# Running sums of a softmax layer in banks taken per segment, VectorE exponentials from key tile 7 on, and transposes by DMA in the last layer

## The chip, the cores and the metric

The kernel runs on one core of a Trainium2 chip. The metric is device time in microseconds (us) from the first to the last instruction's end, the median of several executions. The core's engines are TensorE (PE; its weight loads are listed as PEld), VectorE (DVE), ScalarE (ACT), GpSimd (POOL) and SyncE (SP), which here only issues DMAs.

## What is computed

The input x has 2048 tokens of 512 features in bf16. Four layers follow each other, A, B, A, B, each with its own layer normalisation and a residual. A is softmax attention with 32 query heads of 16 features and a single key and value head. B is linear attention with 32 heads.

```python
def _A_ref(x, wq, wk, wv, wo):
    q = (x @ wq).reshape(B, S, H, Dh).transpose(0, 2, 1, 3)
    k = x @ wk
    v = x @ wv
    p = _softmax(jnp.einsum("bhqd,bkd->bhqk", q, k) * (Dh ** -0.5), axis=-1)
    o = jnp.einsum("bhqk,bkd->bhqd", p, v)
    return o.transpose(0, 2, 1, 3).reshape(B, S, H * Dh) @ wo

def _B_ref(x, wqkv, wo):
    q, k, v = ...                       # 32 heads of 16
    phi = lambda t: jnp.where(t > 0, t + 1, jnp.exp(t)) + 1e-6
    kv = jnp.einsum("bhsd,bhse->bhde", phi(k), v)
    z = phi(k).sum(over s)
    o = (phi(q) @ kv) / (phi(q) @ z + 1e-6)
    return o.reshape(B, S, D) @ wo

x = x + _A_ref(_layernorm(x), ...); x = x + _B_ref(_layernorm(x), ...)
x = x + _A_ref(_layernorm(x), ...); x = x + _B_ref(_layernorm(x), ...)
```

In layers 0 and 2 each has 32 x 2048 x 2048 exponentials, which are the bulk of the work. Layer 1 and layer 3 need a sum over all tokens before any output.

## The kernel before: how it is tiled and what sets the order

**Tiles.** Tokens are cut into 16 tiles of 128. A *block* is 128 keys by 512 (query, head) columns; for a query tile and a parity (`par`) there are 16 key tiles times four row groups j of 32 partitions, 64 blocks. A layer has 16 x 2 x 64 = 2048 blocks.

**Planner.** The class `Planner` (lines 36 to 313) runs once in Python while the program is written. Every operation is given to it with engines, a duration, a priority (lower first) and the buffers that it reads and writes; it plays them in model time, and the order in which it starts them on each engine is the order of that engine's instructions on the chip. There each engine works its list in order and waits for semaphores. Durations, latencies (`DTL` for DMA transposes) and limits on backlogs are constants in lines 340 to 389, so they set an order and not a time. PSUM banks and buffers are handed out by pools, in order of priority of those who wait.

**A block's way.** `act_stream` (line 913) forms groups. A QK matmul writes a block's scores to a bank (`qk_mm`, line 805, its matmul at line 807). Banks 0 to 2 and 3 to 5 are two *sets*. ScalarE takes two or three blocks of a set in one exponential into one of six `PT` buffers (line 973). VectorE gets single blocks: either the third of a set (`dve_split`, line 1039, when no bank of the pool is free) or one in a bank of its own (`dve_open`, line 1033). It makes an integer approximation of the exponential, one conversion per block (line 1049) and three shifted copies per four blocks (line 1080), whose four value matmuls with weighted values sum up to the exponential. Both functions ask for the flag of key tile `KGATE` (15): before it no block goes to VectorE. `dve_split` also looks at VectorE's planned backlog (`BLS` 1.4, `BLT` 4.0).

**Value rounds.** `pv_try` (line 833) takes up to four finished blocks of different j of the current segment and adds value times exponential to the bank `ACC` = 6 (line 861). A *segment* (`Seg`, line 316) is one query tile and parity with some key tiles: early ones, in `PASSES` and `LATE`, have few key tiles, the later ones all 16. A segment that has all its rounds is copied out by VectorE: `norms` (line 1092) copies or adds bank 6 to `sacc` (lines 1103, 1105), after which the next segment's first round may start. Its rows are then transposed (line 1122), divided (lines 1129, 1133), transposed again (by DMA for query tiles below 12, line 1153) and projected (`epilogue`).

**Pool of banks.** `banks` (line 475) holds 7, then 5, and before the exponentials start also 0 to 4. Bank 5 leaves for a set when key tile 15 exists. Layer normalisation, K, V, Q, norms, projections and `dve_open` share it.

**Filler.** Where TensorE is idle in the plan, `fill` (line 887) and `fill_lin` (line 789) add matmuls with zero or unused result, into the running sum's bank or a spare bank.

**Layers 1 and 3.** Tiles of x go on to layer B as they are done. When all 16 are in, `den` gives the denominators and `main(t)` (line 1370) the outputs: numerators on TensorE (line 1416), division on VectorE into `OB` (line 1420, `NOB` = 4 buffers), transposes of `OB` on TensorE (line 1435), the copy to `OTB` on ScalarE or VectorE (line 569), the projection (line 575) and the residual on VectorE (line 1448). `FARM` lists tiles whose transposes go by DMA (line 1427; none), `RESA` tiles whose residual is added by a matmul with the identity and copied by ScalarE (lines 1443 to 1445; none). In layer 3 `store` (line 1465) sends each tile out. Transposes and stores are all issued by SP.

The start of exponentials and the wait for keys, as they are:

```python
yield ("flag", ("K", L, 0))
yield ("flag", ("K", L, 1))
yield ("flag", ("Q", L, 0))
...
while any(("K", L, kt) not in pl.flags for kt in sg.kts) or ("Q", L, sg.t) not in pl.flags:
```

## Time and profile before

| what | value |
|---|---|
| three runs | 1558.03, 1553.24, 1557.19 us; median 1557.19 |
| the profiled execution's own time | 1556.79 us |
| its span | 1555.1 us, mean granted TensorE clock 0.996 |
| first exponential of layer 0 | at 13.65 us |
| last exponentials of layer 0 and first of layer 2 | about 736 and 759.5 us |
| key tiles 0 to 3 of layer 2 written, 4 to 7, last | about 756 to 775, 805, 869.9 us |
| last exponential of layer 2 | about 1507.5 us |
| layer 3's outputs (numerators to the last residual) | 1520.9 to 1552.7 us |

How to read the profile. Busy time is the time in which an engine ran an instruction. A group's line gives the line of the kernel, the engine, the operation, its output and input with shape, the count, then busy time and the mean of one in ns, and after the second bar the idle time of the engine just before such instructions and what ended it. In the busy time by stretch the columns are the stretch, its length, the busy time (and count) of PE, PEld, DVE, ACT and POOL, the granted clock of TensorE as a share of full speed, the share of DMA and GB/s. In a timeline the columns are start and duration in us, then the instruction, and in brackets how long the engine was idle before it and what it waited for. SPq is the queue of SP.

### The profile page before, as it was taken

The page shows a single profiled execution, that of the slowest core. Times are in us where ns is not written, and L with a number is a line of the kernel's source. Part 1 is how long each engine was busy: PE and PEld are TensorE (multiplying, and loading weights), DVE is VectorE, ACT ScalarE, POOL GpSimd, SP SyncE. Part 2 cuts the span into 40 slices and gives each one's busy share as a digit, 9 for nine tenths or more (in the row PEclk, how much of TensorE's full clock was granted, in tenths as well). Part 3 has the DMA queues.
Part 4 walks back from the last instruction along what each step waited for, and adds up shares of the span by engine and source line. Part 5 has one row for each costly group of instructions (what it writes and reads, how often), then busy time and mean ns, then how long its engine had stood idle before and what let it go on. Part 6 is the DMA issues. An engine that isn't in the chain of part 4 may idle for free.

```text
span 1555.1 us, 36056 instructions
## 1 busy us (share of the span) xinstructions
PE 1458.7 (94%) x14602; PEld 535.4 (34%) x14713; DVE 1448.3 (93%) x2707; ACT 1476.8 (95%) x1500; POOL 68.8 (4%) x122
## 2 busy tenths in 40 slices
PE   8998999999999999999999989999999999999999
PEld 4322332333333333333644323323333333333345
DVE  7999999999999999998676799999999999999977
ACT  8999999999999999999699999899999999999982
POOL 4000000000000000000111000000000000000000
PEclk9999999999999999999999999999999999999998
DMA  5100010000000000000000000000000000000001
GB/s 132 47 2 1 8 22 5 8 8 5 8 8 8 5 8 5 1 1 1 2 1 1 1 1 15 15 8 8 6 9 5 8 8 8 5 5 2 1 2 55
DMA packets 40435, 17.55 MB, mean 11 GB/s; under 512 B 34128, under 2 KB 39760, under 8 KB 40272
## 3 DMA queue, kind: packets, MB, share of 16 engines
q1 hardware_dynamic: 40272, 15.25, 4.2%
q8 instruction: 118, 1.93, 0.5%
q14 instruction: 45, 0.37, 0.1%
HBM read 5.28 MB, written 2.10 MB: 5 GB/s over the span
## 4 chain that ended last, share of the span: by engine, by line
PE 32%; issue 23%; DVE 23%; ACT 20%; POOL 1%; DMA 0%; SPq 0%; ACTq 0%; POOLq 0%; DVEq 0%
ACT PT L973 19%; DVE FB L1049 11%; PE ps L861 11%; PE ps L807 9%; DVE FB L1080 6%; PE ps L575 4%; PE ps L906 2%; PE ps L732 2%; PE ps L1122 1%; POOL rs L655 1%; DVE st L651 1%; DVE sacc L1103 1%; PE ps L793 1%; ACT phE L1205 1%; DVE xn L658 1%
## 5 line engine op out<-in xcount | busy, mean ns | idle before, releaser
L973 ACT ACTIVATE PT<-ps 128x1024 bf16<-128x1024 f32 (+1 forms) x1361 | 1424.5, 1180 | 19.9 <-PE ps L861 13.4
L1049 DVE TENSOR_SCALAR FB<-ps 128x512 int16<-128x512 f32 x1017 | 675.0, 686 | 23.5 <-PE ps L807 20.7
L807 PE MATMUL ps<-QT,KM 32*128 32x512 bf16 x4096 | 533.4, 384 | 46.8 <-ACT PT L973 27.9
L861 PE MATMUL ps<-FB,VW 128*32 128x512 bf16 x4068 | 530.4, 385 | 19.5 <-ACT PT L973 9.5
L861 PE MATMUL ps<-PT,V 128*32 128x512 bf16 x3079 | 513.0, 386 | 9.7 <-ACT PT L973 5.6
L1080 DVE TENSOR_SCALAR FB<-FB 128x2048 int16<-128x2048 int16 (+1 forms) x765 | 503.0, 683 | 0.9
L807 PEld LDWEIGHTS ps<-QT,KM 32*128 32x128 bf16 x4096 | 139.8, 91 | 445.3 <-ACT PT L973 203.8
L861 PEld LDWEIGHTS ps<-FB,VW 128*32 128x32 bf16 x4068 | 133.4, 94 | 219.5 <-issue 113.0
L861 PEld LDWEIGHTS ps<-PT,V 128*32 128x32 bf16 x3079 | 125.9, 94 | 111.8 <-issue 56.1
L906 PE MATMUL ps<-QT,V 128*32 128x512 bf16 (+6 forms) x568 | 131.0, 315 | 0.9 <-DVE FB L1049 0.9
L655 POOL TENSOR_TENSOR rs<-ve,mhalf 128x1 f32<-128x1 f32 x64 | 51.7, 811 | 1398.9 <-DVE ve L653 1386.0
L575 PE MATMUL ps<-wqkv,xnT 128*128 128x512 bf16 (+1 forms) x211 | 65.1, 368 | 3.9 <-issue 2.9
L906 PEld LDWEIGHTS ps<-QT,V 128*32 128x32 bf16 x568 | 44.1, 95 | 59.6 <-issue 39.3
L1103 DVE COPY sacc<-ps 128x512 f32<-128x512 f32 x64 | 43.8, 684 | 7.8 <-PE ps L861 7.6
L1205 ACT ACTIVATE phE<-ps 128x512 bf16<-128x512 f32 (+1 forms) x66 | 41.3, 625 | 6.6 <-PE ps L732 4.7
L1122 PE MATMUL ps<-identF,sacc 128*128 128x128 f32 x256 | 45.9, 291 | 1.5 <-DVE sacc L1103 0.8
L732 PE MATMUL ps<-xnT,wqkv 128*128 128x128 bf16 x512 | 44.3, 221 | 0.0
L651 DVE BATCH_NORM_STATS2 st<-x_sb 128x6 f32<-128x512 bf16 x60 | 40.8, 683 | 2.6 <-DMA x_sb<-in_A_x_dram 2.3
L1105 DVE TENSOR_TENSOR sacc<-sacc,ps 128x512 f32<-128x512 f32 x56 | 38.2, 682 | 2.4 <-PE ps L861 2.1
L732 PE MATMUL ps<-xnT,wq 128*128 128x128 bf16 x480 | 38.6, 224 | 0.0
L575 PEld LDWEIGHTS ps<-wqkv,xnT 128*128 128x128 bf16 x272 | 21.8, 97 | 44.9 <-issue 34.2
L732 PEld LDWEIGHTS ps<-xnT,wqkv 128*128 128x128 bf16 x512 | 29.1, 98 | 22.8 <-issue 19.4
(115 smaller groups left out, 671.1 us busy)
## 6 DMA issues: line engine op xcount, KB each, us to landing
out_dram<-x_sb SPq DMA_DIRECT2D x16, 128.0 KB, 1.7
x_sb<-in_A_x_dram SPq DMA_DIRECT2D x3, 512.0 KB, 6.1
wqkv<-in_B_wqkv_dram SPq DMA_DIRECT2D x1, 1536.0 KB, 7.5
xnT<-xn SPq DMA_TRANSPOSE x36, 2.4
x_sb<-in_A_x_dram SPq DMA_DIRECT2D x4, 128.0 KB, 2.2
wq<-in_A_wq_dram SPq DMA_DIRECT2D x1, 512.0 KB, 4.2
wo<-in_A_wo_dram SPq DMA_DIRECT2D x1, 512.0 KB, 4.1
wo<-in_B_wo_dram SPq DMA_DIRECT2D x1, 512.0 KB, 8.5
```

The lines of the kernel that those rows point to most:

```text
L575: return e.matmul(dst, lhsT=l, rhs=r, start=(k == 0), stop=(k == len(pairs) - 1))
L655: op({PO: (0.55, lambda e: e.tensor_tensor(out=rs[:, t:t + 1], in0=ve[:, t:t + 1], in1=mhalf[:], op=ALU.pow))}, reads=[("ve", t), "mhalf"] ...
L732: ins = e.matmul(dst[:, g * P:(g + 1) * P], lhsT=lhs(g, k), rhs=rhs(k), start=(k == 0), stop=(k == FT - 1))
L807: return e.matmul(bank(b), lhsT=KM[r, sg.par, kt * P:(kt + 1) * P], rhs=QT[r, sg.t, :], start=True, stop=True)
L861: ins = e.matmul(ps[32 * j:32 * j + 32, ACC * 512:(ACC + 1) * 512], lhsT=V[:, kt, :] if w is None else VW[:, kt, w, :], rhs=ap, start=(k = ...
L906: o = op({PE: (n / 2400.0, lambda e: e.matmul(ps[32 * j:32 * j + 32, b * 512:b * 512 + n], lhsT=V0[:], rhs=QT[:, sg.t, 0:n], start=st, sto ...
L973: ex = op({AC: (0.05 + 0.4267 * n, lambda e, n=n, s_=s_, p_=p_: e.activation(PT[:, p_, 0:n * 512], ps[:, s_ * 512:(s_ + n) * 512], ACTF.Ex ...
L1049: o = op({DV: (0.60, lambda e: e.tensor_scalar(out=dst.bitcast(I16), in0=bank(b), scalar1=VB, scalar2=VLO, op0=ALU.add, op1=ALU.max))}, wr ...
L1080: o = op({en: (du, lambda e, w=w, g_=g_: e.tensor_scalar(out=FB[:, g_, 0:n].bitcast(I16), in0=FB[:, f_, 0:n].bitcast(I16), scalar1=float(w ...
L1103: o = op({DV: (0.6, lambda e, src=src: e.tensor_copy(src, bank(ACC)))}, writes=[B_(ACC), key], prio=0.0, lat=0.15)
L1122: o = op({PE: (0.12, lambda e, c=c: e.transpose(ps[:, b * 512 + c * P:b * 512 + (c + 1) * P], src[:, c * P:(c + 1) * P], identF[:]))}, rea ...
L1205: op({AC: (0.07 + n / 1200.0, lambda e: e.activation(phE[:, i, 0:n], bank(b, n), ACTF.Exp))}, reads=[B_(b)], writes=[("phE", i)], prio=min ...
```

## The change

- `ACC` is gone. Bank 6 joins the pool `banks`. Each segment has its own `acc`, which `norms` takes from the pool at priority 0.2 when the segment before has at most `LOWV` = 12 value matmuls left (flag `low`) and the one before that has been copied out (flag `out`). `drain` copies it out and gives the bank back.
- `pv_try` builds a round out of finished blocks of two successive segments, in up to two banks. `fill` may write in either; `fill_lin` needs a free bank for which nobody waits.
- `KGATE` is 7 instead of 15. `act_stream` no longer waits for key tile 1 at the start, and per block for that block's key tile only, not for all of the segment.
- `DTL` is 2.7 instead of 4.0 and `BLT` 3.0 instead of 4.0.
- In layer 3 tiles 1 to 15 transpose by DMA, with buffers in `FB` in place of the four of `OB` and `OTB`, and odd tiles add the residual on TensorE and copy on ScalarE.
- For tile 15 in layers 1 and 3 the value part yields to the key part (`pr + 0.001` and a sleep of 0).

```diff
+LOWV = 12
-DTL = 4.0
+DTL = 2.7
-FARM = {1: (), 3: ()}
+FARM = {1: (), 3: tuple(range(1,16))}
-BLT = 4.0
+BLT = 3.0
-KGATE = 15
-RESA = {1: (), 3: ()}
+KGATE = 7
+RESA = {1: (), 3: tuple(range(1, 16, 2))}
...
-    ACC = 6
-    banks = Pool_([7] + list(GROW) + [b for b in SB if b not in GROW])
+    banks = Pool_([7, 6] + list(GROW) + [b for b in SB if b not in GROW])
...
     def fill_lin():
-        if lin["a"] or pl.busy[PE] or ("x", 3, T - 1) in pl.flags:
+        if lin["a"] or pl.busy[PE] or ("x", 3, T - 1) in pl.flags or not banks.free or banks.wait:
...
         def pv_try():
...
+            open_ = [s for s in segs[cur["i"]:cur["i"] + 2] if s.acc is not None and s.submitted < s.total]
             items, js = [], set()
-            for x in sg.ready:
-                if x[1] not in js and ("V", L, x[0]) in pl.flags:
-                    items.append(x)
-                    js.add(x[1])
+            for s in open_:
+                for x in s.ready:
+                    if x[1] not in js and ("V", L, x[0]) in pl.flags:
+                        items.append((s, x))
+                        js.add(x[1])
...
-                    ins = e.matmul(ps[32 * j:32 * j + 32, ACC * 512:(ACC + 1) * 512], lhsT=V[:, kt, :] if w is None else VW[:, kt, w, :], rhs=ap,
+                    ins = e.matmul(ps[32 * j:32 * j + 32, s.acc * 512:(s.acc + 1) * 512], lhsT=V[:, kt, :] if w is None else VW[:, kt, w, :], rhs=ap,
...
+            s = open_[0]
+            if s.total - s.submitted <= LOWV:
+                pl.flag(("low", L, s.i))
...
         def act_stream():
             yield ("flag", ("K", L, 0))
-            yield ("flag", ("K", L, 1))
             yield ("flag", ("Q", L, 0))
...
-                    while any(("K", L, kt) not in pl.flags for kt in sg.kts) or ("Q", L, sg.t) not in pl.flags:
-                        yield ("flag", next((("K", L, kt) for kt in sg.kts if ("K", L, kt) not in pl.flags), ("Q", L, sg.t)))
-                    else:
-                        group.append((sg,) + blk)
-                        continue
-                    sg.left.insert(0, blk)
-                    break
+                    for f in (("K", L, blk[0]), ("Q", L, sg.t)):
+                        while f not in pl.flags:
+                            yield ("flag", f)
+                    group.append((sg,) + blk)
...
         def norms():
+            yield ("flag", ("Q", L, 0))
+            yield ("flag", ("K", L, 0))
             for sg in segs:
-                pl.flag(("acc", L, sg.i))
+                if sg.i:
+                    yield ("flag", ("low", L, sg.i - 1))
+                if sg.i > 1:
+                    yield ("flag", ("out", L, sg.i - 2))
+                sg.acc = yield ("acq", banks, 0.2)
                 pl.at(pl.now, pv_kick)
+                pl.process(drain(sg))
+
+        def drain(sg):
+            yield ("flag", ("pv", L, sg.i))
+            if sg.i:
+                yield ("flag", ("out", L, sg.i - 1))
...
+            if sg.first:
+                o = op({DV: (0.6, lambda e, src=src: e.tensor_copy(src, bank(sg.acc)))}, writes=[B_(sg.acc), key], prio=0.0, lat=0.15)
+            else:
+                o = op({DV: (0.6, lambda e, src=src: e.tensor_tensor(out=src, in0=src, in1=bank(sg.acc), op=ALU.add))},
+                       writes=[B_(sg.acc), key], prio=0.0, lat=0.15)
+            if sg.last:
+                pl.process(norm(sg, src, key, a_))
+            pl.give_after(banks, sg.acc, [o])
+            pl.flag(("out", L, sg.i))
+            if sg.i == len(segs) - 1:
+                lin["a"] = False
...
         def crit_v(t, sl, pr):
-            bs = yield from acq2(pr)
+            bs = yield from acq2(pr + 0.001)
...
             if t in ECRIT:
                 pl.process(crit_k(t, sl, pr))
+                yield ("sleep", 0.0)
                 yield from crit_v(t, sl, pr)
...
+            if L == 3:
+                i = NOB + t
+                ob, otb = FB[:, t // 4, t % 4 * 512:t % 4 * 512 + 512], FB[:, 4 + t // 4, t % 4 * 512:t % 4 * 512 + 512].rearrange("p (g c) -> p g c", c=P)
+                fo, ft_ = [("FB", t // 4, t % 4)], [("FB", 4 + t // 4, t % 4)]
+            else:
+                i = yield ("acq", ob_pool, pr)
+                ob, otb, fo, ft_ = OB[:, i, :], OTB[:, i, :, :], [], []
...
             if t in FARM[L]:
-                dmat(OTB[:, i, :, :], OB[:, i, :], [("OB", i, 0), ("OB", i, 1)], [("OTB", i)], pr)
+                dmat(otb, ob, [("OB", i, 0), ("OB", i, 1)], [("OTB", i)], pr, after=ft_)
```

## The prediction

> **What bounds the kernel now.** I read the page's busy table and costliest groups first, then the busy time by stretch, then the waits of ScalarE, then the tail in order of time. The execution took 1556.79 us (span 1555.1); the median of the three runs is 1557.19, so the working below stands 0.4 us under the median.
>
> ```profile
> PE 1458.7 (94%) x14602; PEld 535.4 (34%) x14713; DVE 1448.3 (93%) x2707; ACT 1476.8 (95%) x1500; POOL 68.8 (4%) x122
> L973 ACT ACTIVATE PT<-ps 128x1024 bf16<-128x1024 f32 (+1 forms) x1361 | 1424.5, 1180 | 19.9 <-PE ps L861 13.4
> L1049 DVE TENSOR_SCALAR FB<-ps 128x512 int16<-128x512 f32 x1017 | 675.0, 686 | 23.5 <-PE ps L807 20.7
> L1080 DVE TENSOR_SCALAR FB<-FB 128x2048 int16<-128x2048 int16 (+1 forms) x765 | 503.0, 683 | 0.9
> ```
>
> Three engines are nearly full. The exponentials of both softmax layers are 4096 blocks of 128x512: ScalarE did 3079, VectorE 1017. A ScalarE block costs 1424.5/3079 = 0.463 us. A VectorE block costs (675.0+503.0)/1017 = 1.158 us, because it is converted once and shifted three times (four blocks per shift). Together they do 1/0.463 + 1/1.158 = 3.02 blocks per us, ScalarE 71% of them. So **a microsecond of ScalarE idle costs 0.71 us, one of VectorE idle 0.29 us, and a block moved into idle time saves 1/3.02 = 0.33 us**. These are the prices below; they hold while either engine can take any block.
>
> ```profile
> 29.50:39.60 10.10, 9.21 (x106) 4.59 (x109) 7.07 (x21) 10.10 (x10) 4.30 (x10) 1.00 0.58 166
> 806.00:870.00 64.00, 60.17 (x619) 27.77 (x625) 42.97 (x97) 63.48 (x58) 7.53 (x16) 1.00 0.01 1
> 970.00:1070.00 100.00, 94.83 (x913) 30.91 (x921) 99.40 (x184) 94.52 (x99) 3.60 (x4) 1.00 0.06 9
> 1520.80:1532.00 11.20, 10.98 (x95) 6.93 (x96) 6.63 (x10) 1.66 (x3) 0.00 (x0) 0.57 0.04 13
> 1541.00:1549.90 8.90, 8.85 (x80) 5.45 (x79) 8.68 (x17) 1.94 (x4) 0.00 (x0) 1.00 0.26 88
> ```
>
> Columns: stretch, length, busy PE, PEld, DVE, ACT, POOL, granted clock, DMA. In 806 to 870 ScalarE is full and VectorE idles 21.0 us: that is layer 2 before its last key tile exists. In 970 to 1070 VectorE is full and ScalarE loses 5.5 us. In the tail TensorE is full, at a clock of 0.57 at first.
>
> **Overlapping value rounds.** Now one bank holds the running sum: a segment's last value matmuls wait for late VectorE shifts, then VectorE copies the bank out, and only then may the next segment's value matmuls start. The worst place, in order of time:
>
> ```profile
> 972.68 1.04 PE L906 MATMUL ps<-QT,V 128*32 128x512 bf16 x4
> 973.97 0.69 DVE L1105 TENSOR_TENSOR sacc<-sacc,ps 128x512 f32<-128x512 f32 x1
> 974.72 0.40 PE L861 MATMUL ps<-FB,VW 128*32 128x512 bf16 x3
> 975.38 1.02 ACT L973 ACTIVATE PT<-ps 128x1024 bf16<-128x1024 f32 x1 [3.29 <-PE ps L861]
> ```
>
> TensorE plays filler (L906), the copy-out runs, value matmuls follow at once, and ScalarE, whose six result buffers were full, starts 3.29 us late. All such waits are the 13.4 us beside L973. With a second bank taken when 12 value matmuls of the old segment are left, the next segment's rounds go on. At full effect that is 13.4 x 0.71 = 9.5 us; at none 0. I take two thirds, **6.4 us**, since the longest ones have just this form and the short ones may be ordinary queueing. The copy-outs (0.68 us each, 120) stay. What is late next is a QK matmul: VectorE waits 20.7 us for L807, worth 5.9 us if all went; I count none of it.
>
> **VectorE from key tile 7 on.** Layer 2's key tile 7 is written at about 805.5, tile 15 at 869.9. The first limit is VectorE's idle time: three quarters of 21.0 us over 1.158 is 13.6 blocks. The second is TensorE, which idles 3.8 us there and fills 0.8: each such block adds three value matmuls at (530.4+513.0)/7147 = 0.146 us busy, so 10.5 blocks; a packed round of four starts every 0.215 us, which would allow 28. I take 12 blocks: **4.0 us** (0 to 6.0). Layer 0 has 3.0 us of idle VectorE at 29.5 to 39.6, two blocks, **0.7 us**. These blocks queue ahead of layer 1's VectorE work (0.5 before 1.5 and up); that work only has to bring key tiles 8 to 15 in time, and layer 2 then has 256 blocks ready on key tiles 0 to 7, of which about 100 are used by 806, so ScalarE does not run dry.
>
> **Starting on the first key tile.** ScalarE's first exponential starts at 13.65, though key tile 0 was ready at 9.1 and the first queries at 10.6; the start waited for tile 1. Four blocks need tile 0 only: 4 x 0.463 x 0.71 = 1.3 us per layer at most. They stand in ScalarE's queue before copies that layer 0 needs at 11.8 and layer 2 at 757 to 759, so I take half for both, **1.3 us** (-1 to 2.6).
>
> **The tail.** Per pair of tiles TensorE's part of the chain that ended last is 1.83 (projections) + 0.45 (transposes) + 0.45 (numerators) + 0.16 (filler) = 2.89 us:
>
> ```profile
> 1540.47 0.45 PE ps L1435 x8
> 1540.91 0.45 PE ps L1416 x8
> 1541.36 0.16 PE ps L793
> 1541.52 1.83 PE ps L575 x8
> ```
>
> SP's own instructions, min/median/max in ns, are these:
>
> ```profile
> L583 SPq DMA_TRANSPOSE OT<-Osb x24: 1189/1190/2209, 173.9 to 1337.1; - x24
> L1467 SPq DMA_DIRECT2D out_dram<-x_sb x16: 332/332/1102, 1527.6 to 1552.7; - x16
> ```
>
> After: no transposes and no need of filler, but one matmul with the identity for the odd tile (0.22): 1.83 + 0.45 + 0.22 = 2.50. Saved 0.39 x 7.5 pairs = 2.9 us. VectorE falls from 0.42 + 1.28 + 1.44 = 3.1 us of work per pair to 2.0. New is SP's queue, which the planner counts at 0.1 us each: 15 transposes at 1.19 and 16 stores at 0.33 are 23.2 us. Stores queue behind transposes whose tile is not ready, and later transposes behind stores. From the second tile's numerators at 1523.5 SP would end at 1546.7, before today's last store at 1552.7, so it does not set the end, but each first projection waits 2.4 us for a landing instead of one 0.59 us copy. I take off 0.9 us: **2.0 us** (4.6 if SP paced the end, -7 in a rival below).
>
> **Counted at nothing.** The DMA latency of 2.7 instead of 4.0 only reorders; transposes land in 2.4. The VectorE backlog limit of 3.0 instead of 4.0 is covered by VectorE being 95 to 99% busy; each per cent of idle it made over 1400 us would cost 14 x 0.29 = 4.1 us. The order of tile 15's K and V evacuations moves tenths. Filler now needs a free bank with nobody waiting; where that fails, the clock is at stake.
>
> Sum: 6.4 + 4.0 + 0.7 + 1.3 + 2.0 = 14.4; 1556.8 - 14.4 = **1542.4 us**.
>
> **Rivals.**
> - *All stalls go* (0.17): 9.5 + 6.0 + 0.7 + 2.6 + 4.6 and the 5.9 us of QK waits, 29.3, gives **1527.5**. For it: the same stalls feed each other. Against: TensorE is at 94%.
> - *The order does not overlap in fact* (0.13): the instruction order is fixed from the planner's durations, which are short (0.60 against 0.664 for L1049), so the stalls stay and TensorE admits few extra blocks: 2.0 + 0.7 + 0.6 is left, **1553.5**.
> - *The tail stays at half clock* (0.07). The clock drops to 0.50 at 1523 and recovers at about 1532, after projections ran without a gap. At half clock eight projection matmuls took 3.43 us; a tile is then 1.72 + 0.45 + 0.22 = 2.4 us, 16 of them 38 against today's 31: the tail loses 7 and the time is **1551.4**. A proof against it: projections, once fed, fill TensorE at that clock (2.4 us per tile against 1.5 from SP), as in the stretch that ended the drop before. The Trainium skill, TensorE: Matmul & The Clock Gate, "Why this matters for your kernels", warns of idle gaps above about 3 us between bursts of matmuls, each returning the clock to half. This trace dropped with TensorE 98% busy, on matmuls 8 columns wide, so a busy share alone does not rule it out; by that rule a wait for transposes would count too, and the sum would be 1551.4 instead of 1542.4.
> - *Bank shortage* (0.17), the slower one. After a layer's last query tile only banks 6 and 7 serve everything but exponentials. While both hold running sums, norms, output projections and the next layer's K, V and Q wait. ScalarE's groups of two (1004 of 1361) are formed mostly when bank 7 is not free, so it is taken some 70% of the time; of the 45 us per token tile 13.5 are spare. It decides once two sums overlap for over 13.5/2 = 6.7 us per segment (the case above shows 4). Then the next layer falls a tile behind: K, V and Q of a tile take 2.5 + 1.5 + 2.8 = 6.9 us, twice 13.7. With the overlap's gain gone, 1556.8 + 13.7 - 8.0 = **1562.5**.
>
> **Chances.** Forecast 0.46, the rivals as given. A difference under 0.3% (4.7 us) cannot be told from none here. Faster: 0.46 + 0.17 + 0.03 of the second and 0.03 of the third = 0.69; same 0.14; slower 0.17. The range, 1527 to 1562, reaches from the full gain to the shortage and leaves out about half of each.
>
> **What would show it.** Overlap right: idle of L973 before value matmuls falls from 13.4 to about 4 us, and less filler. Key gate right: L1049 from about 806 on, VectorE over 85% busy in 806 to 870, some 14 more VectorE blocks in all. Tail right: no L1435 but for tile 0, about 2.5 us per pair, the last store near 1538. Wrong: copy-outs of running sums late with idle ScalarE behind them, a longer stretch between layers, transposes on SP back to back up to the end, or a clock of 0.5 beyond ten microseconds.

## The result, and the profile after

The changed kernel takes 1563.22 us (median of 20 runs, 1555.18 to 1570.17), the kernel before in the same series 1556.49 (20 runs, 1552.34 to 1558.06). The ratio is 1.0046, 95% interval 1.0032 to 1.0059: **slower by 6.7 us**, where 14.4 us less had been forecast. The profiled execution took 1562.38 us (span 1560.5, mean granted clock 0.991; before 1555.1 and 0.996).

What the change was to do, it did. From the page, the busy table and the groups of the exponentials (in the order of the lines shown of before):

```profile
PE 1477.1 (95%) x14568; PEld 532.9 (34%) x14676; DVE 1455.5 (93%) x2723; ACT 1474.9 (95%) x1538; POOL 70.7 (5%) x122
L967 ACT ACTIVATE PT<-ps 128x1024 bf16<-128x1024 f32 (+1 forms) x1398 | 1418.4, 1135 | 11.7 <-PE ps L807 6.5
L1043 DVE TENSOR_SCALAR FB<-ps 128x512 int16<-128x512 f32 x1034 | 688.3, 684 | 24.1 <-PE ps L807 20.2
L1074 DVE TENSOR_SCALAR FB<-FB 128x2048 int16<-128x2048 int16 x780 | 513.2, 678 | 0.7
```

VectorE did 17 blocks more (1034 for 1017). ScalarE's idle time before exponentials fell from 19.9 to 11.7 us, and value matmuls, which had been behind 13.4 of it, are behind 3.6 in its waits:

```profile
ACT PT L967 <- PE ps L807: 6.5, 17, 0.8
ACT PT L967 <- PE ps L857: 3.6, 9, 0.9
```

The same stretches as before, by engine (length, PE, PEld, DVE, ACT, POOL, granted clock, DMA): VectorE now works 55.61 us of 806 to 870 (42.97 before), and in 970 to 1070 ScalarE is full (99.83, 94.52 before).

```profile
806.00:870.00 64.00, 61.03 (x546) 21.86 (x548) 55.61 (x113) 62.13 (x67) 7.13 (x11) 1.00 0.01 1
970.00:1070.00 100.00, 98.57 (x998) 34.72 (x997) 98.39 (x182) 99.83 (x99) 2.71 (x3) 1.00 0.07 12
1520.80:1532.00 11.20, 10.96 (x109) 7.79 (x110) 7.97 (x13) 0.59 (x1) 0.00 (x0) 0.53 0.38 68
```

Where the gain went is seen by cutting the two executions at the same events, in us:

| event | before | after | part's change |
|---|---|---|---|
| last exponential of layer 0 ends | 736.2 | 730.9 | -5.3 |
| first exponential of layer 2 | 759.5 | 756.7 | +2.5 |
| last exponential of layer 2 ends | 1507.98 | 1498.7 | -6.5 |
| first denominator of layer 3 | 1519.12 | 1520.10 | **+10.3** |
| end of the span | 1555.1 | 1560.5 | **+4.4** |

Up to layer 0's last exponential and within layer 2's exponentials, 11.8 us are saved in this execution, where 12.4 were forecast for overlap, gate and start. That the two agree is luck. The experiments e1, e2, e13 and e18 below have the changed kernel's order of instructions in layer 0, and there its last exponential ends at 736.4 to 737.5 us, later than before. What repeats is the stretch from the 200th of layer 0's 2048 blocks to the last: 639.5 to 640.5 us in these five executions, 645.0 before. The first 200 blocks took 90.8 us here but 96.4 to 97.7 in the other four (91.2 before). And part of layer 2's 6.5 us is work put off: the stretch behind its exponentials is 10.3 us longer, and layer 3's outputs lose 4.4 more.

ScalarE behind layer 2's last exponential, in order of time, first after:

```profile
1487.86 10.84 ACT L967 ACTIVATE PT<-ps 128x1024 bf16<-128x1024 f32 x10
1498.55 0.63 ACT L1271 CAST va<-ps 128x512 bf16<-128x512 f32 x1
1500.83 0.60 ACT L1212 ACTIVATE phE<-ps 128x512 bf16<-128x512 f32 x1 [1.65 <-PE ps L732]
...
1506.56 1.16 ACT L1212 ACTIVATE phE<-ps 128x512 bf16<-128x512 f32 x2
...
1513.58 0.60 ACT L1212 ACTIVATE phE<-ps 128x512 bf16<-128x512 f32 x1 [1.50 <-PE ps L732]
1515.33 1.64 ACT L1212 ACTIVATE phE<-ps 128x256 bf16<-128x256 f32 x4 [1.16 <-DVE QT L1215]
1516.83 0.68 ACT L1243 CAST va<-ps 128x256 bf16<-128x256 f32 x2
1517.87 0.60 ACT L1212 ACTIVATE phE<-ps 128x512 bf16<-128x512 f32 x1 [0.35 <-PE ps L732]
```

and before, where four such operations (L1205 there) are all that is left:

```profile
1494.20 13.77 ACT L973 ACTIVATE PT<-ps 128x1536 bf16<-128x1536 f32 x12
1507.77 0.69 ACT L1263 CAST va<-ps 128x512 bf16<-128x512 f32 x1
1510.82 0.60 ACT L1205 ACTIVATE phE<-ps 128x512 bf16<-128x512 f32 x1 [2.36 <-PE ps L732]
```

`phE` is the feature map of layer 3's queries and keys, one operation per tile for each and two for the last tile's keys; the queries' matmul (L732) needs a bank. In the changed kernel 8 of these operations fall in 760 to 1300 (20 before) and 15 behind 1490 (4 before), where no exponentials hide them. Of layer 3's 16 query tiles 13 come behind the last exponential, 2 before.

What lengthens the outputs is, as e13 will show, the work of SP, whose list holds the transposes and the stores of layer 3 in one order:

```profile
1524.03 5.64 SPq L583 DMA_TRANSPOSE FB<-FB  x4
1529.76 0.54 SPq L1482 DMA_DIRECT2D out_dram<-x_sb  x1
1530.39 1.19 SPq L583 DMA_TRANSPOSE FB<-FB  x1
1533.54 4.46 SPq L1482 DMA_DIRECT2D out_dram<-x_sb  x4
1538.27 5.00 SPq L583 DMA_TRANSPOSE FB<-FB  x3
1543.36 0.53 SPq L1482 DMA_DIRECT2D out_dram<-x_sb  x1
1543.94 6.43 SPq L583 DMA_TRANSPOSE FB<-FB  x5
...
1554.28 3.96 SPq L1482 DMA_DIRECT2D out_dram<-x_sb  x8
```

Five transposes have gone by 1531.6. Then four stores stand first in the list and wait for projections, which run at a clock of 0.53 in 1520.8 to 1532; the other ten transposes come behind them, from 1538.27 on: ten at 1.19 us and three stores at 0.53 are 13.5 of the 15.9 us up to 1554.2, so hardly a pause is left.

### The profile page after: what moved, and what is told of

It is laid out like the page before. It is cut to its first block, busy times and chain, and to the rows that moved or that the text cites. A ratio compares the mean times of both kernels' runs of the same rounds, so it can differ in the third digit from the quotient of the medians.

```text
span 1560.5 us, 36074 instructions
## 1 busy us (share of the span) xinstructions
PE 1477.1 (95%) x14568; PEld 532.9 (34%) x14676; DVE 1455.5 (93%) x2723; ACT 1474.9 (95%) x1538; POOL 70.7 (5%) x122
## 4 chain that ended last, share of the span: by engine, by line
PE 43%; DVE 22%; ACT 18%; issue 15%; DMA 1%; POOL 1%; SPq 0%; ACTq 0%; POOLq 0%; DVEq 0%
ACT PT L967 17%; PE ps L857 15%; PE ps L807 13%; DVE FB L1043 10%; DVE FB L1074 7%; PE ps L575 4%; PE ps L904 4%; PE ps L732 2%; PE ps L1129 2%; DVE sacc L1108 1%; DMA FB<-FB 1%; POOL rs L655 1%; DVE st L651 1%; DVE QT L1215 1%; DVE sacc L1215 0%
## 5 line engine op out<-in xcount | busy, mean ns | idle before, releaser
L967 ACT ACTIVATE PT<-ps 128x1024 bf16<-128x1024 f32 (+1 forms) x1398 | 1418.4, 1135 | 11.7 <-PE ps L807 6.5
L1043 DVE TENSOR_SCALAR FB<-ps 128x512 int16<-128x512 f32 x1034 | 688.3, 684 | 24.1 <-PE ps L807 20.2
L857 PE MATMUL ps<-FB,VW 128*32 128x512 bf16 x4136 | 581.7, 386 | 12.1 <-ACT PT L967 7.9
L807 PE MATMUL ps<-QT,KM 32*128 32x512 bf16 x4096 | 547.9, 384 | 34.3 <-ACT PT L967 13.6
L857 PE MATMUL ps<-PT,V 128*32 128x512 bf16 x3062 | 548.7, 387 | 9.5 <-ACT PT L967 6.5
L1074 DVE TENSOR_SCALAR FB<-FB 128x2048 int16<-128x2048 int16 x780 | 513.2, 678 | 0.7
L857 PEld LDWEIGHTS ps<-FB,VW 128*32 128x32 bf16 x4136 | 142.1, 94 | 206.3 <-issue 106.7
L904 PE MATMUL ps<-QT,V 128*32 128x512 bf16 (+6 forms) x615 | 164.3, 329 | 0.5 <-issue 0.5
L1212 ACT ACTIVATE phE<-ps 128x512 bf16<-128x512 f32 (+1 forms) x66 | 39.9, 610 | 13.6 <-PE ps L732 9.7
L732 PE MATMUL ps<-xnT,wq 128*128 128x128 bf16 x480 | 41.6, 229 | 0.1
L1462 DVE TENSOR_TENSOR x_sb<-x_sb,ps 128x512 bf16<-128x512 bf16 x22 | 15.1, 685 | 24.3 <-PE ps L575 24.2
L732 PE MATMUL ps<-xnT,wqkv 128*128 128x128 bf16 x512 | 37.1, 220 | 0.1
L575 PEld LDWEIGHTS ps<-wqkv,xnT 128*128 128x128 bf16 x272 | 21.7, 97 | 44.7 <-issue 35.3
```

The source lines that it names most:

```text
L575: return e.matmul(dst, lhsT=l, rhs=r, start=(k == 0), stop=(k == len(pairs) - 1))
L732: ins = e.matmul(dst[:, g * P:(g + 1) * P], lhsT=lhs(g, k), rhs=rhs(k), start=(k == 0), stop=(k == FT - 1))
L807: return e.matmul(bank(b), lhsT=KM[r, sg.par, kt * P:(kt + 1) * P], rhs=QT[r, sg.t, :], start=True, stop=True)
L857: ins = e.matmul(ps[32 * j:32 * j + 32, s.acc * 512:(s.acc + 1) * 512], lhsT=V[:, kt, :] if w is None else VW[:, kt, w, :], rhs=ap, start= ...
L904: o = op({PE: (n / 2400.0, lambda e: e.matmul(ps[32 * j:32 * j + 32, b * 512:b * 512 + n], lhsT=V0[:], rhs=QT[:, sg.t, 0:n], start=st, sto ...
L967: ex = op({AC: (0.05 + 0.4267 * n, lambda e, n=n, s_=s_, p_=p_: e.activation(PT[:, p_, 0:n * 512], ps[:, s_ * 512:(s_ + n) * 512], ACTF.Ex ...
```

## The experiments

All kernels were compared with the kernel before on the same chip. In the table, *half clock* is the mean over a kernel's runs of (1 - granted clock) x time x 2, the time that TensorE would have spent at half speed (without the start, see below the table). *Exponentials* is layer 2 from the first to the last, *gap* from there to the first denominator of layer 3, *outputs* from there to the end; these and the start of layer 2 are of the one profiled execution.

| kernel | median us | ratio to before | half clock | layer 2 starts | exponentials | gap | outputs |
|---|---|---|---|---|---|---|---|
| before | 1556.49 | | 11 | 759.5 | 748.5 | 11.1 | 36.0 |
| after | 1563.22 | 1.0046 [1.0032, 1.0059] | 27 | 756.7 | 742.0 | 21.4 | 40.4 |
| e1 old outputs | 1563.16 | 1.0032 [1.0021, 1.0043] | 28 | 762.6 | 742.2 | 21.5 | 34.7 |
| e2 residual matmul | 1565.33 | 1.0051 [1.0038, 1.0063] | 36 | 762.2 | 741.6 | 21.6 | 35.7 |
| e3 no overlap | 1561.66 | 1.0025 [1.0014, 1.0037] | 32 | 766.5 | 746.9 | 11.6 | 33.7 |
| e4 queries first | 1557.03 | 0.9995 [0.9982, 1.0009] | 17 | 762.3 | 746.3 | 13.6 | 33.0 |
| e5 second key wait | 1558.07 | 1.0015 [1.0002, 1.0028] | 23 | 762.7 | 737.2 | 14.2 | 39.4 |
| e6 queries first, DMA | 1560.50 | 1.0033 [1.0021, 1.0045] | 20 | 766.2 | 746.7 | 13.6 | 37.5 |
| e7 before, gate 7 | 1557.46 | 1.0015 [1.0001, 1.0029] | 13 | 765.6 | 747.2 | 11.1 | 33.3 |
| e8 queries first, key wait | 1558.26 | 1.0010 [1.0001, 1.0020] | 23 | 771.9 | 741.6 | 13.2 | 32.3 |
| e9 more filler | 1564.14 | 1.0052 [1.0032, 1.0072] | 27 | 762.8 | 744.1 | 19.2 | 35.8 |
| e10 e8 and filler | 1557.33 | 1.0012 [1.0001, 1.0022] | 19 | 769.0 | 739.8 | 13.7 | 32.6 |
| e11 queries first, half DMA | 1555.38 | 0.9996 [0.9986, 1.0006] | 14 | 759.8 | 745.8 | 13.7 | 35.3 |
| e12 before, more filler | 1565.32 | 1.0059 [1.0043, 1.0076] | 17 | 769.3 | 744.2 | 11.9 | 35.8 |
| e13 half DMA alone | 1558.29 | 1.0012 [0.9997, 1.0026] | 22 | 763.3 | 742.1 | 21.4 | 30.8 |
| e14 half DMA, key wait | 1556.50 | 0.9995 [0.9982, 1.0008] | 31 | 767.7 | 739.9 | 14.0 | 35.4 |
| e15 all three | 1561.42 | 1.0031 [1.0019, 1.0043] | 23 | 765.4 | 741.9 | 13.1 | 35.2 |
| e16 e11, gate 15 | 1577.26 | 1.0128 [1.0109, 1.0147] | 38 | 765.0 | 766.9 | 13.7 | 31.9 |
| e17 e11, one bank | 1556.61 | 1.0009 [0.9991, 1.0026] | 26 | 761.7 | 750.7 | 11.7 | 35.2 |
| e18 e13, one bank | 1546.96 | 0.9952 [0.9930, 0.9975] | 21 | 762.1 | 734.7 | 18.0 | 30.8 |

Differences between two experiments are given below as differences of ratios, times 1556.5 us. By the intervals of the two ratios such a difference is uncertain by some 3 us (4 with e9, e12, e17 and e18), so a smaller one cannot be told from none.

The trace's record of the clock begins with its first change, to the full clock, and what lies before counts as full in the column. That is up to 8.9 to 13.2 us in thirteen of the twenty profiled executions (10.4 before, 9.5 after), and up to 17.2 to 27.5 us in e1, e2, e3, e11, e16, e17 and e18. Until then matmuls take as long as at half clock: in all twenty a 128x128 matmul has a median of 314 ns there and 219 ns at full clock. The QK matmuls of 12 to 24 us, before and in e1, both in a window listed with a clock of 1.00:

```profile
L807 PE MATMUL ps<-QT,KM 32*128 32x512 bf16 x24 | 3.9, 384 | 0.2
L807 PE MATMUL ps<-QT,KM 32*128 32x512 bf16 x15 | 3.5, 605 | 0.0
```

In the kernel before such a matmul takes 602 ns where the granted clock is 0.50 (at 24.7 us). Over the twenty executions the time of layer 0's first 200 blocks goes with the half-clock time up to 80 us, the start counted in (correlation 0.84, 0.26 us per us). These blocks take 90.8 to 94.3 us in the kernel before, e7, e12 and the changed kernel's one execution, and 95.0 to 102.4 in all others.

**The theories.** The first was that of the prediction's slower rival: with both banks held by running sums, layer 3's queries wait for a bank and are late (shortage). Against it stood that they lack time on TensorE, and that the outputs alone are to blame.

### The outputs: e1, e2, e6, e11, e13

```diff
e1:  -FARM = {1: (), 3: tuple(range(1,16))}      +FARM = {1: (), 3: ()}
     -RESA = {1: (), 3: tuple(range(1, 16, 2))}  +RESA = {1: (), 3: ()}
e2:  FARM as in e1, RESA as in the change
e6:  the change, and in q_:  +b = yield ("acq", banks, 0.1)
e11: e6, and  +FARM = {1: (), 3: tuple(range(1,16,2))}
e13: the change, and  +FARM = {1: (), 3: tuple(range(1,16,2))}
```

> The changed kernel with layer 3's outputs as before: no transposes by DMA there, no residual by matmul. Everything up to the last sum over tokens keeps its order, so only the last 40 us can differ. Theory T (SP paces the tail: 15 transposes of 1.19 us and 16 stores in one list, stores that wait for a projection hold up later transposes): the outputs take 32 to 33 us again instead of 37, the time falls by 4 to 7 us to 1556 to 1559, about level with the kernel before. Rival T2 (the tail is long because the clock is at 0.5 and the layer enters it late, whatever transposes the tiles): less than 2 us of change, 1561 to 1565.

> As the one with the old tail, but odd tiles add the residual by a matmul with the identity and ScalarE copies the result; transposes stay on TensorE. Theory T: within 1 us of the old tail, 1556 to 1559, since VectorE loses 8 additions of 0.68 us and TensorE gets 8 matmuls of 0.22 us. If the residual matmuls were the tail's cost: 1561 or more, as the changed kernel.

> The changed kernel with the queries served first for a bank, as in the run before, but with its transposes by DMA and residual matmuls in the outputs: it differs from that kernel in the tail alone, which the run of the old tail could not settle because layer 0 had come out 6 us later there at another clock. Theory T (the 15 transposes of 1.19 us and 16 stores of 0.53 us in SP's one in-order list pace the outputs): first denominator to end 38 to 42 us where the old tail took 33.0, and 1561 to 1564 in the median. Rival (the outputs stretched in the changed kernel only because the late queries and the clock stood in their way): 33 to 35 us and 1557 to 1558.

> The changed kernel with the queries first for a bank and only the odd tiles of the outputs (8 instead of 15) transposed by DMA; the residual matmuls stay. Theory T (SP's list paces the outputs): SP has 8 of 1.19 us and 16 of 0.53 us, 18 us in sum instead of 26, and no longer paces; first denominator to end is 32 to 35 us instead of the 37.5 of the run with all 15 by DMA, and the median 1556 to 1559 against its 1560.5. Rival (what costs is the way of a single DMA transpose, some 2 us from issue to landing, or the residual matmuls on TensorE): 36 to 38 us and 1559.5 to 1562.

> The changed kernel with one edit: only the odd tiles of the outputs are transposed by DMA. If the prices add up (outputs 5.1 us, from 1560.5 to 1555.4 where the queries were first): 1557.5 to 1559.5 from 1563.2, with the queries still late (10 or more phi exponentials behind 1490 us, 18 to 22 us between the last exponential and the first denominator). Rival (the late queries hide the outputs' list, since SP can work ahead while TensorE catches up): 1561 to 1564.

With the old outputs (e1) these take 34.7 us instead of 40.4, but the ratio falls by 2.2 us only, which cannot be told from none (4 to 7 had been forecast): in that execution layer 2 began 5.9 us later, with the same order of instructions up to there, and TensorE came to the full clock at 25.3 us only. The residual matmul alone (e2) is not faster than e1 (+3.0 us, the intervals overlap). The clear pairs are those with all and with half of the transposes on SP: after and e13, -5.3 us (outputs 40.4 to 30.8), and e6 and e11, -5.8 us; from all of them to the old outputs it is -5.9 us (e6 to e4).

Part of the 40.4 us is the clock: the changed kernel's outputs hold 13.7 us at half clock, those before 10.2. In seven executions no matmul of the outputs ran at half clock. They took 32.3 to 33.0 us with the old outputs (e4, e8, e10), 35.8 and 37.5 with all transposes on SP (e9, e6), and 30.8 with half of them (e13, e18). SP's list in e13 has pauses again, as in the first of these rows, whose three stores take longer than the three of the last:

```profile
1544.99 2.83 SPq L1482 DMA_DIRECT2D out_dram<-x_sb  x3
1547.91 1.20 SPq L583 DMA_TRANSPOSE FB<-FB  x1
1549.15 1.54 SPq L1482 DMA_DIRECT2D out_dram<-x_sb  x3
```

So the 15 transposes in SP's list lengthened the outputs, which these pairs show at 5.3 to 5.9 us. That each DMA transpose costs by its own way would be a rival, but with 8 of them, and the residual matmuls, the outputs are shorter than with none. With half of the transposes the changed kernel stands at 1.0012 [0.9997, 1.0026], not told apart from before.

### The late queries: e3, e4

```diff
e3: e1, and  -LOWV = 12   +LOWV = 0
e4: e1, and in q_:  -b = yield ("acq", banks, pr)   +b = yield ("acq", banks, 0.1)
```

> The old tail, and the second running sum is asked for only when the first has all its value matmuls (limit 0 instead of 12), so two banks are held for the copy-out alone. Theory S (bank shortage: two running sums leave layers 1 and 3 no bank, their queries fall behind and are made up after the exponentials): at most 5 phi exponentials of layer 3 after layer 2's last softmax exponential instead of 15, the stretch from that exponential to the first denominator falls from 21.6 to about 12 us; the exponentials of layer 2 end 5 to 9 us later than in the changed kernel; time 1553 to 1558. Rival P (TensorE has no time left for the low priority of queries, because of VectorE's extra blocks from key tile 7 on): 10 or more of the phi exponentials stay late, 20 us or more, 1560 or more.

> The old tail and the full overlap, but a query tile of layers 1 and 3 asks for its bank at priority 0.1, ahead of the running sums (0.2); its matmuls keep their low priority on TensorE. Theory S: the queries come in time, at most 5 phi exponentials late, and the catch-up stretch falls to about 12 us; the exponentials end later by what the running sums wait, 4 to 8 us, so the time is 1552 to 1558. Rival P: the queries hold a bank and still wait for TensorE; they stay late and the running sums are late too, 1562 or more.

Both shorten the gap, to 11.6 and 13.6 us. The `phE` operations of the changed kernel and then of e4 (columns: stretch, length, ScalarE busy with these alone, clock, DMA):

```profile
760.00:1300.00 540.00, 5.13 (x8) 0.99 0.03 7
1490.00:1525.00 35.00, 8.17 (x15) 0.95 0.01 1
```

```profile
760.00:1300.00 540.00, 9.70 (x15) 1.00 0.03 7
1490.00:1525.00 35.00, 3.88 (x7) 1.00 0.01 2
```

e4 changes nothing but who gets a bank first, and behind the last exponential 3 of layer 3's query tiles are left, where e1 has 13 (e3: 1): the shortage of banks made them late, not TensorE's time. Its price is not the gap, though. The exponentials grow from 742.2 to 746.3 us, so some 4 of 8 us are paid elsewhere, and that much of the changed kernel's gain in layer 2 was queries put off. e4 against e1 is -5.8 us, part of it at the clock (17 us of half clock for 28). And where other edits had been made, serving the queries first gained less or lost: -2.0 us (after to e6) and -2.5 (e13 to e11), neither of which can be told from none, +5.6 (e14 to e15), +8.9 (e18 to e17).

e3's time missed its range of 1553 to 1558. Without the overlap ScalarE waits 12.0 us for value matmuls again (3.8 in e1), and layer 0's 200th to last block take 647.2 us (640.5 in e1). So the overlap does shorten the exponentials, and what it gains there goes in the gap.

### The early start and the opening of layer 2: e5, e8, e14, e15, e17, e18

```diff
e5:  the change, and in act_stream:  +yield ("flag", ("K", L, 1))
e8:  e4 and that line;  e14: e13 and that line;  e15: e11 and that line
e18: e13, and in norms:
-    yield ("flag", ("low", L, sg.i - 1))
+    yield ("flag", (("pv" if L == 2 and sg.i < 16 else "low"), L, sg.i - 1))
e17: e11 and that line
```

> The changed kernel with one line put back: the exponentials wait for the second key tile again before they start. Open is why the changed kernel runs longer at half TensorE clock: over 20 runs each, its granted clock stands for 27 us at half speed per run (before: 11), and time over half-clock time has a slope of 0.24 to 0.32 us per us. Theory C (the early start): the exponentials' start switches the idle-time filler of the opening (L793) off 3 us earlier, TensorE is then thinly used from 10 us on and the clock falls in 10 to 60 us. Then this kernel stands at 10 to 16 us of half clock per run and at 1559 to 1560, 3 to 4 us under the changed kernel. Theory B (the filler between the value matmuls, which may only write a running bank or a free one): the half-clock time stays at 24 to 30 us and the time at 1561 to 1564. In the model of the planner its queries of the last layer are as late as in the changed kernel, so the 21 us between the last exponential and the first denominator stay under both.

> The changed kernel with the old outputs, the queries served first for a bank (as in the run at 1557.03) and the wait for the second key tile put back: what stays of the change is the overlap of the value rounds and the VectorE exponentials from key tile 7. Theory C (the early start costs the clock): half-clock time 8 to 12 us per run where the same kernel without the wait had 17, and 1553 to 1556: faster than before by 2 to 4 us. Theory B (the filler): 15 to 20 us and 1557 to 1559, since the exponentials start 1.3 us later.

> The changed kernel with half of the outputs' transposes by DMA and the wait for the second key tile put back; the queries wait for a bank as in the change. If prices add up (start 5.1 us, from 1563.2 to 1558.1; outputs 5.1): 1552 to 1554.5, faster than before. Rival (the run with the key wait had merely drawn another order of the queues, in which fewer queries were late): 1556 to 1560.

> The changed kernel with all three edits: queries first for a bank, the wait for the second key tile, half of the outputs' transposes by DMA. If prices added up fully this would stand at 1550 to 1552. But queries first with old outputs was 1557.0 without the key wait and 1558.3 with it, so the start's price was not there once the queries came first: then 1555 to 1557.5.

> The kernel with queries first for a bank and half of the outputs' transposes by DMA (1555.4), with one more edit: for the first 16 segments of layer 2 a segment takes its bank only when all value matmuls of the one before are submitted, so that the running sums hold one bank there and the overlap is off. Theory K (two held banks delay the keys of the opening): the last keys by 895 to 905 us instead of 924, more VectorE blocks in 870 to 930, and 1551 to 1554: below both kernels. Rival (the keys wait for something else, and the ScalarE waits for the value matmuls come back in the opening): last keys at 910 or later, and 1555 to 1559.

> The changed kernel with half of the outputs' transposes by DMA (1558.3) and the overlap off for the first 16 segments of layer 2, with the queries as the change has them. Theory K: the last keys by 895 to 905 us instead of some 910, and 1554 to 1557, with the last layer's queries still late (18 to 22 us to the first denominator). Rival: 1558 to 1561.

Layer 2 starts 2.8 us earlier in the changed kernel, since layer 0 ended earlier (from there it is 2.5 us later), and then runs dry. ScalarE from 764 us on, after:

```profile
763.80 7.86 ACT L967 ACTIVATE PT<-ps 128x1024 bf16<-128x1024 f32 x7
772.08 0.17 ACT L569 CAST V<-ps 128x16 bf16<-128x16 f32 x1 [0.41 <-PE ps L575]
773.41 0.59 ACT L569 CAST QT<-ps 128x512 bf16<-128x512 f32 x1 [1.16 <-PE ps L732]
776.05 0.59 ACT L569 COPY OTB<-ps 128x512 bf16<-128x512 bf16 x1 [2.06 <-PE ps L1449]
778.97 0.59 ACT L569 COPY xnT<-ps 128x512 bf16<-128x512 bf16 x1 [2.33 <-PE ps L678]
780.17 0.17 ACT L569 CAST V<-ps 128x16 bf16<-128x16 f32 x1 [0.61 <-PE ps L575]
781.69 0.47 ACT L720 ACTIVATE KM<-ps,kmask 128x256 bf16<-128x256 f32 x1 [1.35 <-PE ps L575]
```

Between 771.7 and 781.7 there is no exponential. ScalarE waits 7.9 us for one matmul after another of layer 1's outputs and layer 2's inputs, up to keys 2 and 3 (L720, its line 781.69); before, these keys were written at 774.3 and the exponentials went on. Busy time of 765 to 800 us, before, after, and e18:

```profile
765.00:800.00 35.00, 33.59 (x338) 14.84 (x339) 26.16 (x63) 34.66 (x32) 4.83 (x10) 1.00 0.01 1
```

```profile
765.00:800.00 35.00, 31.40 (x276) 13.82 (x278) 22.71 (x52) 27.04 (x29) 4.75 (x10) 0.95 0.01 2
```

```profile
765.00:800.00 35.00, 32.17 (x301) 13.59 (x299) 22.25 (x53) 32.84 (x33) 4.15 (x9) 1.00 0.01 2
```

ScalarE idles 0.3, 8.0 and 2.2 us. Two different edits cure this hole: the wait for the second key (1.3 us of idle in e5) and one running sum in the opening (e18, overlap off for its 16 segments; e13, the same kernel without that, idles 8.7). What the cure brings in the end is not settled. The key wait gave -4.8 us (e5), -2.6 (e14), +2.3 (e8), +5.4 (e15), of which -2.6 and +2.3 cannot be told from none. In e5 and e14 it also left 8 query tiles behind the last exponential instead of 13, so their gain is not that of the hole alone. e15 fits neither of its forecasts. The one bank gave **-9.3 us in e18, which is faster than both kernels** (0.9952 [0.9930, 0.9975]), and +2.0 in e17 (the intervals overlap), though the last keys came earlier in both (909 for 919 and 924). Theory K asked for 895 to 905; e17's time is the rival's, e18's is below either forecast. In e3, without the overlap, the last keys come at 908, so two held sums are not what delays most of them; what does stays open. e17's runs also had 26 us of half clock where e11's had 14. The reason given for e5, that the early start costs clock time, fell: the half-clock time was 23 us there, not 10 to 16, and rose from 17 to 23 in e8.

### The gate of VectorE: e7, e16

```diff
e7:  the kernel before, and  -KGATE = 15  +KGATE = 7
e16: e11, and  -KGATE = 7   +KGATE = 15
```

> The kernel before with one constant changed: VectorE exponentials from key tile 7 on instead of 15. The prediction gave this 4.0 us in layer 2 and 0.7 in layer 0. If it holds alone: some 14 more blocks of VectorE exponentials, 20 or more of them in 806 to 870 us instead of 2, and 1551 to 1554. Rival (the order of the queues is written out anew from the change on, and its chance effects are as large as the gain): the blocks come, but the time is 1556 to 1561; the gap between the last exponential and the first denominator, or the clock, then shows what took it back.

> The kernel with queries first and half of the outputs' transposes by DMA (1555.4), with the VectorE exponentials from key tile 15 on again. What the gate is worth with the overlap: the prediction gave 4.7 us, so 1559 to 1561 and some 14 to 20 fewer VectorE blocks, next to none of them in 806 to 870 us. Rival (as in the kernel before, where the gate alone gave nothing): 1554.5 to 1557.

Alone the gate gives nothing, and with the overlap its loss costs 20.5 us (e11 to e16; the latter has 24 us more of half clock in it), not 4.7. Stretch 806 to 870, e7 and then e16:

```profile
806.00:870.00 64.00, 61.94 (x611) 25.94 (x618) 57.59 (x117) 59.81 (x67) 8.62 (x13) 1.00 0.01 2
```

```profile
806.00:870.00 64.00, 61.38 (x505) 22.35 (x502) 33.30 (x74) 63.15 (x57) 6.50 (x14) 0.98 0.00 1
```

In e7 VectorE fills the stretch (57.59 us for 42.97), but ScalarE falls from 63.48 to 59.81: it waits 2.6 us for value matmuls (0.2 before), since one bank holds the running sum. As far as these two kernels show, the gate needs the overlap. In e16 VectorE gets no block before 900, because key tile 15 comes at 913 us there; it came at 869 in the kernel before, and at 913 in the changed kernel too. The change delays layer 2's last keys by 44 us, and the early gate keeps VectorE at work meanwhile (55.61 us in 806 to 870, 33.30 in e16).

### The filler: e9, e10, e12

```diff
-lv + WORK * (self.now - t) / 3.413
+lv + (8192 if self.now < 70 or 735 < self.now < 830 else WORK) * (self.now - t) / 3.413
e9: the change;  e10: e8;  e12: the kernel before
```

> The changed kernel with the quota of the idle-time filler (WORK) raised from 5000 to 8192 columns per 3.413 us in the two openings (planned time under 70 us and 735 to 830 us); all else as changed. In the traces so far each fall of the granted clock in 10 to 65 us comes right behind a stretch of 2 us in which TensorE was busy for only 1.36 to 1.67 us, and it then lasts 3 to 27 us. Theory G (gaps of TensorE in the openings set off the half clock): more filler in the openings closes them, half-clock time falls from 27 us per run to 18 or less, and the median from 1563 to 1558 to 1560. Rival H (the gaps are waits of TensorE's in-order queue that a planned filler cannot fill, or the clock does not follow them): half-clock time stays at 23 to 30 us and the time at 1561 to 1564, or above that, where the added matmuls delay others.

> The kernel with old outputs, queries first for a bank and the wait for the second key tile (1558.26 with 23 us at half clock; its fit of time against half-clock time gives 1551.7 at full clock) with the same raised filler in the openings. Theory G: half-clock time 5 to 12 us and 1553 to 1555, below the kernel before. Rival H: 18 to 25 us and 1557 to 1560.

> The kernel before with the same raised filler in the openings, as a control: what the filler is worth without the change. Theory G: its half-clock time falls from 11 us per run to 6 or less and its median by 1 to 2 us to 1555 to 1556.5. Rival H: unchanged at 10 to 12 us, 1556.5 to 1559.

The half-clock time did not fall: 27 us as in the change, 19 for 23, and 17 for 11 in the kernel before, which became 9 us slower. But the edit did not do what it was written for, so theory G is not tested by it. The quota is a credit without an upper limit, and what an opening did not use was spent behind it. Up to 75 us the filler matmuls are as many as without the edit (7 of L906 and 35 of L793 in e12 and before; 21 and 35 in e10 and e8) or fewer (e9). Filler grew between the openings instead, where the clock does not fall in any of these traces. L906 from 75 to 735 us, before and e12:

```profile
L906 PE MATMUL ps<-QT,V 128*32 128x512 bf16 (+6 forms) x242 | 59.2, 327 | 0.3 <-DVE FB L1049 0.3
L906 PE MATMUL ps<-QT,V 128*32 128x512 bf16 (+4 forms) x291 | 85.5, 363 | 0.6 <-issue 0.3 <-DVE FB L1049 0.2
```

In that stretch ScalarE waits 10.9 us for value matmuls in e12 (2.9 before), so there filler is not free. With the overlap it was: in e9 it grows from 71.3 to 88.0 us, and layer 0's 200th to last block take 640.6 us, for 640.1 in the changed kernel.

## Why the prediction was wrong

- **Overlap (6.4 us): the mechanism right, the size not measured alone.** The waits of ScalarE for value matmuls fell from 13.4 to 3.6 us, as forecast (about 4), and layer 0's 200th to last block take 5 us less in five executions. In the whole time e3 without it and e1 with it are not told apart (1.0025 and 1.0032), since the late queries take it back.
- **Gate (4.0 and 0.7): the blocks right, the reason not.** 17 blocks more against 14; VectorE at 87% in 806 to 870. But the working took layer 2's keys where they stood before. They moved 44 us back, and the gate alone was worth nothing (e7).
- **The step that failed first: the sum had no term for the next layer.** "While both hold running sums, norms, output projections and the next layer's K, V and Q wait" stood in the slower rival, at a chance of 0.17 and a price of 13.7 us, with 1562.5 as its result. The gap behind layer 2 grew by 10.3 us. The rival's mechanism is the one that e3 and e4 show; its sum went wrong in that it took the exponentials' gain for lost, while they did end 9.3 us earlier in the profiled execution (by e4 some 4 of that is queries put off), and in leaving the outputs out. So its 1562.5 is near the 1563.2 measured by luck in the sum.
- **The tail: the sign failed, forecast 2.0 saved, measured 4.4 lost.** The step was "SP would end at 1546.7, before today's last store at 1552.7, so it does not set the end". It summed SP's durations from the first tile on as if none waited. Transposes stood behind stores that waited for projections, a store between transposes took 0.53 us instead of 0.33, and the last one ended at 1558.2. "4.6 if SP paced the end" was counted as a further gain, without a working; against the old outputs it was a loss of 5.9 us (e6 to e4), and of 3 to 5 in the outputs that ran at full clock. Of the 4.4 in the table a part is the clock.
- **Early start (1.3, bound -1 to 2.6): the bound too narrow.** The first exponentials came 2.8 us earlier in both layers, but in layer 2 only because layer 0 had ended 5.3 earlier. Layer 2's ran dry 15 us later, and 8.0 us of ScalarE in 765 to 800 went, for 0.3 before. That copies "stand in ScalarE's queue" was seen, but not that the blocks of the first keys would be used up before keys 2 and 3 exist.
- **Filler, "counted at nothing": not covered.** Half-clock time rose from 11 to 27 us per run, the start not counted. By the fits below a microsecond of it goes with 0.24 to 0.33 us, so 4 to 5 us of the difference. These are no sum beside the table's: the half clock lies inside the parts, mostly in the two openings and the outputs.
- **The order is planned anew with every edit.** The same line moved the time by -9.3 and +2.0, or -4.8 and +5.4 us, in kernels that are near each other. A chance effect of some 5 us either way belonged in the range on top of the costs; it would have held the result.

What stays open: why the changed kernel and nearly all its variants stand longer at half clock, why the full clock first comes at 9 us in one execution and at 25 in another, what delays layer 2's last keys, and how much of e18's gain is the opening and how much a lucky order. Only the transposes on SP showed the same price more than once.

## What to carry to other kernels

When a second buffer is given to the engine that sets the pace, ask first who else was living from that pool, and follow the work that waits to the place where nothing hides it: here the next layer's queries and keys, 10.3 us behind the last exponential. Sum an in-order DMA list together with what each of its entries waits for, and not its durations alone. In a kernel whose order is planned as a whole, trust an effect only when it appears in two neighbouring kernels with the same sign, and count in the trace whether an edit did what its line says before a theory is dropped on it.

## What the runs showed of the hardware

A run's time follows its granted clock. Over the 131 runs of the kernel before in the experiments, time against half-clock time has a slope of 0.33 us per us (correlation 0.94) and stands at 1552.9 us at full clock; over 20 of the changed kernel 0.24 (0.85) and 1556.4; over the ten of e18 0.41 (0.90). In e1 and e11 there is none (-0.03 over 6 runs, -0.04 over 12); there the start, which the half-clock time leaves out, lasted 25.3 and 23.7 us in the profiled execution. In the twenty profiled executions the recorded clock is 0.50 or 1.00, and each fall ahead of the last matmul lasts a multiple of some 3.4 us, from 3.4 to 27.3. The Trainium skill, TensorE: Matmul & The Clock Gate, section "Terms", puts the penalty at the throttled time times the lost share, which would be 0.5 per us; these fits lie under it. A reason that fits, but that no run isolates, is that other engines set the pace for part of the time: TensorE has 43% of the chain that ended last in the changed kernel.

A fall can last long while TensorE is busy. In e8, with ScalarE down to 19.62 us of 27:

```profile
34.00:61.00 27.00, 25.76 (x138) 5.69 (x141) 16.59 (x30) 19.62 (x21) 3.62 (x6) 0.50 0.29 98
```

TensorE is busy for 25.76 of 27 us, all at half clock. The same page, section "What's actually happening", lets the full clock return after some 3.4 us of sustained work. This row does not agree with that as far as busy time is a measure of sustained work; the busy time of matmuls is modelled in the profile, so short gaps inside it may be hidden.
